# Pooling additions cut into pieces on GpSimd, and contiguous additions in place of strided sums on VectorE

## The chip, the core and the metric

One core of one Trainium2 chip runs the kernel. The metric is the device time of one execution in microseconds (us), as the median of several runs. Three runs of the kernel before gave 667.07, 664.21 and 663.7 us: median 664.21. Engines are named as in the profile: PE (TensorE matmul), PEld (its weight load), DVE (VectorE), ACT (ScalarE), POOL (GpSimd), SP (SyncE, which issues most of the DMAs).

## What is computed

An attention with pooled keys and values (8 batches, 8 heads, 576 rows, head size 64), and behind it a mixture of eight experts of which each row uses one:

```python
k_p = k.reshape(B, H, 72, 8, D).mean(axis=3)          # 576 keys -> 72 means of 8
v_p = v.reshape(B, H, 72, 8, D).mean(axis=3)
attn = softmax(q @ k_p.T / sqrt(D)); out = attn @ v_p
x = out as 4608 rows of 512
e = argmax(x @ w_gate); gate = softmax(x @ w_gate)[e]; eom = sigmoid(x @ w_output_gate)[e]
y = gate * eom * (relu(x @ w1[e]) @ w2[e])
```

The change concerns only the two `mean` lines: how the sums over eight neighbours are made.

## The kernel before

The program has two phases. In the first (`attention_and_routing`, up to about 180 us) the 4608 rows go through in 36 tiles of 128 rows, each in two half-steps `a` of four heads. All engines work as a software pipeline that is written out by hand: the main loop at L520 and below emits, for tile `i` and half `a`, the scores of tile `i` (PE, L228), the transposes of the probabilities of tile `i-2` (PE, L248), the row maxima `m` (DVE, L234), the products with the values of tile `i-3` (PE, L256), the exponentials (ACT, L239) and the normalising of tile `i-3` (DVE, L273, L279, L281). Each engine executes its own list in this order. In the second phase (`experts`, to the end) loops over the experts multiply rows by weights on PE.

A batch has 576 rows, so 4.5 tiles. For each batch `b` after the first, a table of due steps (`at(...)`, around L490) says when its side work is put into the lists: the keys are loaded (SP), pooled on POOL by `pool_k` (L170) and scaled by ACT (L179); the values are loaded into the one buffer `vt` (a part of `rows`; SP, L158), halved on POOL by `halve_v` (L185, at L188: the eight summands of 64 elements become four), then summed on DVE by `pool_v` (L190, at L191), placed by ACT (L201) and turned by PE (L206). The DVE part of the pooling goes through a queue of small steps: `pooled(b)` is a generator, and `work(n)` takes up to `n` steps from the queue's front at three places of a half-step (2, 1 and 1 steps, `WORK`). Behind it in the same queue stand the routing steps of a group of four tiles (`route`, L296 to L357): small DVE instructions on 128x32 or 128x4 elements in SBUF, among them L302, L306, L310, L314, L331 and L334, with matmuls `rk` between them. POOL's own list holds, besides the pooling, the scatters of finished rows (L390) and a few small fills.

For batch 0 nothing is halved: `first_v` has DVE sum eight summands at once, and DVE also pools its keys (`ready_k`). The list of DVE at the start is therefore keys half 0, values half 0, `m`, keys half 1, values half 1, `m`.

`vt` exists once, so SP's loads of the next values wait until DVE (or POOL) has read the old ones.

Of the kernel before, what the change touches and what calls it, by code (L numbers as in the profile page):

```python
# [15 lines left out]
ALU = mybir.AluOpType  # L16
AX = mybir.AxisListType
PSUM = bass.MemoryType.PSUM

B, H, S, D = 8, 8, 576, 64  # L20
# [49 lines left out]
def attention_and_routing(ctx, tc, sh, qT, kT, v, wg, wst, xs):  # L70
    nc = tc.nc
# [12 lines left out]
    vt = sh.rows[:, 0:6 * DM].rearrange("p (a c f) -> p a c f", a=2, c=3)  # L84
# [61 lines left out]
    k_t, vp_t, vT_t = {}, {}, {}  # L146
# [20 lines left out]
        nc.sync.dma_start(k_t[0][:, 2:4], k[:, 2:4])  # L167
        nc.sync.dma_start(q_t[0][:, :, P:S], q[:, :, P:S])

    def pool_k(b, eng, c0=0, c1=4):  # L170
        k = k_t[b][:, c0:c1]
        for w in (4, 2):
            eng.tensor_tensor(k[:, :, 0:w], k[:, :, 0:w], k[:, :, w:2 * w], op=ALU.add)
        eng.tensor_tensor(k[:, :, 0], k[:, :, 0], k[:, :, 1], op=ALU.add)

    def scale_k(b, c0=0, c1=4):
        for h in range(2):
# [3 lines left out]
    def ready_k(a):  # L181
        pool_k(0, nc.vector, 2 * a, 2 * a + 2)
        scale_k(0, 2 * a, 2 * a + 2)

    def halve_v(b):  # L185
        vp_t[b] = p2.tile([P, 3, 2, D], F32, tag="vp", name=f"vp{b}", bufs=1)
        for a in range(2):
            nc.gpsimd.tensor_tensor(vt[:, a, :, 0:256], vt[:, a, :, 0:256], vt[:, a, :, 256:512], op=ALU.add)  # L188

    def pool_v(b, a, c, n=1, w=4):  # L190
        nc.vector.tensor_reduce(vp_t[b][:, c:c + n, a], vt[:, a, c:c + n, 0:w * D].rearrange("p c (r d) -> p c d r", r=w),  # L191
                                axis=AX.X, op=ALU.add)

    def first_v(a):
        if a == 0:
            vp_t[0] = p2.tile([P, 3, 2, D], F32, tag="vp", name="vp0", bufs=1)
        pool_v(0, a, 0, 3, 8)

    def place_v(b, c):
        for h in range(2):  # L200
# [264 lines left out]
    def at(step, f, *args):  # L465
        plan.setdefault(step, []).append((f, args))

    def pooled(b):
        for a in range(2):
            for c in range(3):  # L470
                pool_v(b, a, c)
                yield 0

    tick = [0]
# [15 lines left out]
    for b in range(1, B):  # L490
        f = S * b // P + 0.5 * (b % 2)
        at(f - 8.5, load_k, b)
        at(max(f - 5, 0), load_v, b)
        at(f - 4.5, load_q, b)
        at(f - 5.5, pool_k, b, nc.gpsimd)
        at(max(f - 2.5, 1.5), scale_k, b)
        at(f - 2.5, halve_v, b)
        at(f - 2, lambda b: queue.insert(0, [pooled(b), 0, -1]), b)
        for c in range(3):
            at(f - 0.5 + 0.5 * c, place_v, b, c)  # L500
        at(f - 0.5, turn_v, b)
        at(f + 1.5, gate_v, b)
# [18 lines left out]
    prepare_counts()  # L521
    ready_k(0)
    first_v(0)
    at(-0.5, ready_k, 1)
    at(-0.5, first_v, 1)
    at(1.5, prepare_routing)
    for c in range(3):
# [603 lines left out]
def program():  # L1131
# [12 lines left out]
    with ExitStack() as st:  # L1144
# [27 lines left out]
        with tile.TileContext(nc) as tc:  # L1172
            with ExitStack() as ctx, tc.manual_schedule():
                attention_and_routing(ctx, tc, sh, qT, kT, v, wg, wst, xs)
# [24 lines left out]
```

## Time and profile before

| | us |
|---|---|
| median of 3 runs | 664.21 |
| the profiled execution, its own time | 664.95 |
| its span in the trace | 663.2 |
| PE busy in the span | 612.9 (92%) |
| DVE busy | 356.3 (54%) |
| ACT busy | 260.0 (39%) |
| POOL busy | 217.4 (33%) |
| mean granted TensorE clock | 0.98 |

The profiled execution stands 0.74 us above the median of the runs. The shares are means over the whole span; DVE and ACT work mostly in the first phase. A row of the timeline gives start, length, engine, line, operation, output and input, the count of instructions merged into it, and in brackets the idle time of the engine before it and what ended it. A row of the groups gives the count, the busy time and the mean length in ns, then the idle time. A row of the windows gives for a stretch of time each engine's busy time, then the granted TensorE clock, the DMA share and the GB/s.

### The profile page before, as it was taken

The numbers are of one execution on the slowest core, as the hardware profiler recorded it, in microseconds if no ns is written. First come the engines' busy times: TensorE is split into PE (matmuls) and PEld (weight loads), VectorE is DVE, ScalarE is ACT, GpSimd is POOL, SyncE is SP. The second block draws the span as 40 slices with busy tenths as digits, with TensorE's granted clock in tenths as the row PEclk, the third lists the DMA queues.
The fourth block names the chain that finished last, engine by engine and source line by source line (L and its number), as shares of the span: only waits on it lengthen the run. The fifth ranks groups of instructions, "written<-read, shape, count | busy, mean of one in ns | idle before, by whom it ended". The sixth has DMA issues, their size and how long they took to land.

```text
span 663.2 us, 11977 instructions
## 1 busy us (share of the span) xinstructions
PE 612.9 (92%) x3715; PEld 558.4 (84%) x3716; DVE 356.3 (54%) x877; ACT 260.0 (39%) x693; POOL 217.4 (33%) x270
## 2 busy tenths in 40 slices
PE   0898988999978999999999999999998899999996
PEld 0787877988976999899798988999897898989895
DVE  5689989899883722577546422354142722222221
ACT  2776857888541511347244301333040420211110
POOL 3547628663432321231404112131222213030213
PEclk9998988999998899999989999999999899999999
DMA  8899757883435921467746422074113102020203
GB/s 268 275 290 285 225 181 263 251 231 121 129 144 177 315 80 49 122 215 248 272 139 209 149 70 61 19 231 134 55 22 134 32 20 80 16 63 32 64 32 77
DMA packets 28746, 95.82 MB, mean 144 GB/s; under 512 B 4735, under 2 KB 5759, under 8 KB 26882
## 3 DMA queue, kind: packets, MB, share of 16 engines
q1 hardware_dynamic: 18194, 61.92, 29.5%
q0 software_dynamic: 10480, 33.13, 15.1%
q8 instruction: 21, 0.34, 0.2%
q14 instruction: 51, 0.42, 0.2%
HBM read 76.13 MB, written 20.22 MB: 145 GB/s over the span
## 4 chain that ended last, share of the span: by engine, by line
PE 66%; issue 2%; DVE 1%; DVEq 0%; POOL 0%; ACT 0%; POOLq 0%
PE p_y L849 32%; PE p_h L868 31%; PE p_x L830 2%; DVE w1a L993 1%; PE p_y L830 0%; POOL out L1110 0%; DVE rows L999 0%; DVE xt L986 0%; ACT xt L933 0%; PE p_y L910 0%; DVE sums L1019 0%; DVEq L681 0%; DVEq L1018 0%; DVEq L1030 0%; DVEq L798 0%
## 5 line engine op out<-in xcount | busy, mean ns | idle before, releaser
L948 ACT ACTIVATE ht<-p_h 128x384 fp32r<-128x384 f32 (+1 forms) x104 | 46.8, 450 | 267.0 <-PE p_h L868 266.7
L868 PE MATMUL p_h<-xt,w1b 128*128 128x384 f32 (+1 forms) x736 | 117.8, 321 | 4.1 <-issue 3.0
L868 PEld LDWEIGHTS p_h<-xt,w1b 128*128 128x128 f32 x736 | 116.6, 191 | 5.4 <-issue 3.5
L849 PE MATMUL p_y<-w2a,ht 128*128 128x512 f32 x456 | 109.1, 399 | 6.2 <-issue 4.2
L1006 DVE SCALAR_TENSOR_TENSOR ht<-p_h,ht 128x384 fp32r<-128x384 f32 (+1 forms) x104 | 52.5, 505 | 114.9 <-ACT ht L948 114.8
L849 PE MATMUL p_y<-w2b,ht 128*128 128x512 f32 x480 | 113.6, 396 | 0.0
L849 PEld LDWEIGHTS p_y<-w2a,ht 128*128 128x128 f32 x456 | 87.1, 193 | 25.0 <-issue 6.7
L849 PEld LDWEIGHTS p_y<-w2b,ht 128*128 128x128 f32 x480 | 89.8, 188 | 20.5
L868 PE MATMUL p_h<-xt,w1a 128*128 128x256 f32 (+1 forms) x640 | 95.1, 309 | 4.2 <-DVE sums L1019 4.2
L868 PEld LDWEIGHTS p_h<-xt,w1a 128*128 128x128 f32 x640 | 94.4, 193 | 5.0 <-DVE sums L1019 4.4
L999 DVE TENSOR_SCALAR rows<-p_y,sc 128x512 f32<-128x512 f32 x41 | 30.5, 749 | 122.7 <-PE p_y L849 122.7
L1110 POOL DMA_INDIRECT out<-rows,dst x41 | 41.6, 1015 | 129.7 <-DVE rows L999 124.9
L256 PE MATMUL av<-vbd,pT 128*128 128x162 f32 (+1 forms) x480 | 75.6, 313 | 8.5 <-DVE vbd L216 2.9
L239 ACT ACTIVATE p<-p_h,m 128x72 f32<-128x72 f32 x288 | 70.9, 361 | 25.4 <-DVE m L234 25.2
L256 PEld LDWEIGHTS av<-vbd,pT 128*128 128x128 f32 (+1 forms) x480 | 62.8, 185 | 11.9 <-issue 6.4
L1085 POOL DMA_INDIRECT rows<-xs,src x51 | 58.6, 1149 | 24.2 <-POOL src L1081 13.9
L1080 POOL COPY nx<-rows 128x6 f32<-128x6 f32 x17 | 3.2, 190 | 149.1 <-PE p_y L830 71.2
L390 POOL DMA_INDIRECT xs<-xg,where x36 | 36.0, 1000 | 47.2 <-DVE where L345 22.9
L228 PE MATMUL p_h<-kbd,q_even 128*128 128x144 f32 (+1 forms) x160 | 30.6, 321 | 15.7 <-DMA q_even<-qT 12.2
L249 ACT ACTIVATE pT<-ptr 128x384 f32<-128x384 f32 x72 | 37.8, 526 | 5.7 <-PE ptr L248 5.6
L228 PEld LDWEIGHTS p_h<-kbd,q_even 128*128 128x128 f32 (+1 forms) x160 | 24.5, 203 | 17.1 <-issue 12.2
L248 PE MATMUL ptr<-ident,p 128*128 128x128 f32 x216 | 37.2, 283 | 1.8 <-DVE running L333 1.7
(172 smaller groups left out, 712.2 us busy)
## 6 DMA issues: line engine op xcount, KB each, us to landing
stage<-wst SPq DMA_DIRECT2D x64, 512.0 KB, 5.3
kq<-kT SPq DMA_DIRECT2D x7, 1152.0 KB
rows<-v SPq DMA_DIRECT2D x16, 288.0 KB
kq<-qT SPq DMA_DIRECT2D x4, 1152.0 KB
q_even<-qT SPq DMA_DIRECT2D x3, 1152.0 KB
rows<-v SPq DMA_DIRECT2D x8, 256.0 KB
rows<-v SPq DMA_DIRECT2D x8, 160.0 KB
kq<-kT SPq DMA_DIRECT2D x2, 576.0 KB
```

The costliest lines, as they stand in the source:

```text
L228: nc.tensor.matmul(s[r0:r0 + n, 144 * c:144 * c + 144], q_t[b][:, 2 * a + c, s0:s0 + n], kbd[b % 2][:, 2 * a + c, :], start=True, stop=True)
L239: nc.scalar.activation(pt[i % 3][:, 4 * a + h, 0:KEYS], sv[:, h], AF.Exp, bias=m[:, h:h + 1])
L248: nc.tensor.transpose(tr[:, P * c:P * c + P], src[:, o:o + P], ident)
L249: nc.scalar.activation(pT_t[i][:, 3 * a:3 * a + 3, :], tr[:, 0:384].rearrange("p (c n) -> p c n", c=3), AF.Copy)
L256: nc.tensor.matmul(av[r0:r0 + n, COLS * c:COLS * c + 2 * COLS], pT[:, 3 * a + c, r0:r0 + n], vbd[b % 2][:, a, c].rearrange("p h f -> p (h ...
L390: ins = nc.gpsimd.indirect_dma_start(out=xs, out_offset=bass.IndirectOffsetOnAxis(ap=where, axis=0), in_=x.bitcast(I32), in_offset=None)
L849: i = mm(p_y[k], ht[:, h, f, P * k:P * k + P], w[:, part, o:o + DM], start=(f == 0 and part == 0 and h == 0), stop=(f == 7 and h == 1))
L868: i = mm(to, w[:, part, o:o + P], x, start=(d == 0 and k == 0), stop=(d == 3 and k == len(terms) - 1))
L948: act(ht[:, 0, f, 0:size * P], p_h[f % 3][:, 0:size * P], AF.Relu).then_inc(q["hh"], 1)
L1006: nc.vector.scalar_tensor_tensor(ht[:, 1, f, 0:n], src, 0.0, ht[:, 0, f, 0:n].bitcast(F32), op0=ALU.max, op1=ALU.subtract).then_inc(q["hl" ...
L1085: nc.gpsimd.indirect_dma_start(out=xb[:, k].bitcast(I32), out_offset=None, in_=xs, in_offset=bass.IndirectOffsetOnAxis(ap=src[:, k:k + 1], ...
L1110: nc.gpsimd.indirect_dma_start(out=out, out_offset=bass.IndirectOffsetOnAxis(ap=dst[:, k:k + 1], axis=0), in_=yb[k], in_offset=None, bound ...
```

## The change

`pool_k` gets an argument `apart`; with 1 (batches 1 to 7, on POOL) the first two of its three levels are issued for one of the four column groups at a time, 288 and 144 elements in place of 1152 and 576. `halve_v` is issued for each third of the values, 256 elements in place of 768. `pool_v` no longer sums four summands by a strided `tensor_reduce`, three instructions for a half of the heads; it adds contiguous halves of the buffer by two `tensor_tensor` instructions (384 and 192 elements), the first of them in place. `first_v` uses three of these (768, 384, 192 elements). The queue item `pooled(b)` has four steps in place of six.

```diff
-    def pool_k(b, eng, c0=0, c1=4):
-        k = k_t[b][:, c0:c1]
-        for w in (4, 2):
-            eng.tensor_tensor(k[:, :, 0:w], k[:, :, 0:w], k[:, :, w:2 * w], op=ALU.add)
-        eng.tensor_tensor(k[:, :, 0], k[:, :, 0], k[:, :, 1], op=ALU.add)
+    def pool_k(b, eng, c0=0, c1=4, apart=0):
+        for w in (4, 2, 1):
+            n = apart if apart and w > 1 else c1 - c0
+            for c in range(c0, c1, n):
+                k = k_t[b][:, c:c + n]
+                eng.tensor_tensor(k[:, :, 0:w], k[:, :, 0:w], k[:, :, w:2 * w], op=ALU.add)
...
         for a in range(2):
-            nc.gpsimd.tensor_tensor(vt[:, a, :, 0:256], vt[:, a, :, 0:256], vt[:, a, :, 256:512], op=ALU.add)
-
-    def pool_v(b, a, c, n=1, w=4):
-        nc.vector.tensor_reduce(vp_t[b][:, c:c + n, a], vt[:, a, c:c + n, 0:w * D].rearrange("p c (r d) -> p c d r", r=w),
-                                axis=AX.X, op=ALU.add)
+            for c in range(3):
+                nc.gpsimd.tensor_tensor(vt[:, a, c, 0:256], vt[:, a, c, 0:256], vt[:, a, c, 256:512], op=ALU.add)
+
+    def pool_v(b, a, n):
+        to = vt[:, a, :, 0:n] if n > D else vp_t[b][:, :, a]
+        nc.vector.tensor_tensor(to, vt[:, a, :, 0:n], vt[:, a, :, n:2 * n], op=ALU.add)
...
-        pool_v(0, a, 0, 3, 8)
+        for n in (4 * D, 2 * D, D):
+            pool_v(0, a, n)
...
-            for c in range(3):
-                pool_v(b, a, c)
+            for n in (2 * D, D):
+                pool_v(b, a, n)
                 yield 0
...
-        at(f - 5.5, pool_k, b, nc.gpsimd)
+        at(f - 5.5, pool_k, b, nc.gpsimd, 0, 4, 1)
```

In the new file L191 becomes L194, L188 becomes L190, L173 and L174 become L175, and the lines below stand three further down (L331 becomes L334).

First place, POOL's list in the attention phase, from the keys of batch 2 to the values of batch 2 (`kq` are the keys, `rows` the values, `xg` a group's rows). Before:

```order
L173 TENSOR_TENSOR kq<-kq 128x4x288
L173 TENSOR_TENSOR kq<-kq 128x4x144
L174 TENSOR_TENSOR kq<-kq 128x4x72
L268 IOTA xg_499 128x4
L188 TENSOR_TENSOR rows<-rows 128x3x256 x2
```

and now:

```order
L175 TENSOR_TENSOR kq<-kq 128x288 x4
L175 TENSOR_TENSOR kq<-kq 128x144 x4
L175 TENSOR_TENSOR kq<-kq 128x4x72
L271 IOTA xg_517 128x4
L190 TENSOR_TENSOR rows<-rows 128x256 x6
```

Nothing has changed places; five instructions have become fifteen. The 144-element pieces each wait for their own 288-element piece, the last level for all of them; the six pieces of the values wait for nothing that POOL does.

Second place, DVE's list where the values of batch 2 are pooled, in the middle of the routing of the first group (`vp` are the pooled values, `gden` and `pos` belong to the routing, `m`, `grec`, `xg`, `graw` to the tiles). Before:

```order
L234 TENSOR_REDUCE m_0_560<-p_h 128x4
L191 TENSOR_REDUCE vp_517<-rows 128x64 x2
L273 RECIPROCAL grec_501<-av_0_564 128x4
L191 TENSOR_REDUCE vp_517<-rows 128x64
L279 TENSOR_TENSOR xg_499<-av_0_564,grec_501 128x256
L281 TENSOR_TENSOR graw_498<-av_0_564,grec_501 128x64
L191 TENSOR_REDUCE vp_517<-rows 128x64
L234 TENSOR_REDUCE m_1_584<-p_h 128x4
L191 TENSOR_REDUCE vp_517<-rows 128x64 x2
L273 RECIPROCAL grec_501<-av_1_588 128x4
L326 TENSOR_REDUCE gden_599<-ex_489 128x4
```

and now:

```order
L237 TENSOR_REDUCE m_0_582<-p_h 128x4
L194 TENSOR_TENSOR rows<-rows 128x3x128
L194 TENSOR_TENSOR vp_535<-rows 128x3x64
L276 RECIPROCAL grec_519<-av_0_586 128x4
L194 TENSOR_TENSOR rows<-rows 128x3x128
L282 TENSOR_TENSOR xg_517<-av_0_586,grec_519 128x256
L284 TENSOR_TENSOR graw_516<-av_0_586,grec_519 128x64
L194 TENSOR_TENSOR vp_535<-rows 128x3x64
L237 TENSOR_REDUCE m_1_606<-p_h 128x4
L329 TENSOR_REDUCE gden_614<-ex_507 128x4
L333 TENSOR_TENSOR pos_617<-rk_608,running 128x32
```

The pooling of a batch now ends in the half-step in which it begins, and the routing steps behind it stand two steps of the queue earlier. The step that first reads the second half of the heads (the second `rows<-rows`) stands in front of that half-step's `xg`; before, the fourth reduce did, behind `xg`.

## The prediction

> **What bounds the kernel now.** First the windows, to see where the change can matter. It touches the attention phase alone, so I compare that phase with the long one behind it:
>
> ```profile
> 20.00:165.00 145.00, 131.62 (x1028) 120.78 (x1029) 129.55 (x454) 112.35 (x424) 84.91 (x69) 0.96 0.75 238
> 200.00:663.00 463.00, 447.33 (x2474) 405.21 (x2473) 184.76 (x281) 125.89 (x216) 112.36 (x156) 0.98 0.35 112
> ```
>
> From 200 us on PE is busy for 447 of 463 us; nothing there changes, so time saved earlier shifts this part as a whole. From 20 to 165 us PE (first busy figure) and DVE (third) are both nearly full, 131.6 and 129.6 of 145 us. Two full engines do not each cost their whole time: DVE costs only where PE runs dry. The waits of PE in these 145 us show how much that is:
>
> ```profile
> PE av L256 <- DVE vbd L216: 2.9, 1, 2.9
> PE av L256 <- DVE grec__3_1365 L339: 1.9, 1, 1.9
> PE ptr L248 <- DVE running L333: 1.7, 1, 1.7
> PE av L256 <- DVE graw L281: 1.6, 2, 1.1
> PE av L256 <- DVE zr L316: 1.5, 2, 1.1
> ```
>
> These are 9.6 us, all for DVE. They are few and long, so the next question is what DVE did just before. The longest, in the timeline, with the clock granted after it and after two others (the figure before the last two):
>
> ```profile
> 81.11 3.57 POOL L188 TENSOR_TENSOR rows<-rows 128x768 f32<-128x768 f32 x2
> 81.42 3.31 DVE L310 TENSOR_TENSOR oh<-cand,best 128x32 bf16<-128x32 f32 x1
> 85.74 1.04 PE L256 MATMUL av<-vbd,pT 128*64 128x162 f32 x10 [2.91 <-DVE vbd L216]
> 57.00:60.00 3.00, 3.00 (x16) 2.99 (x15) 2.56 (x11) 2.48 (x10) 2.37 (x3) 0.58 1.10 214
> 87.00:90.00 3.00, 3.00 (x22) 2.79 (x23) 1.37 (x6) 2.28 (x8) 0.00 (x0) 0.50 0.27 100
> 111.00:114.00 3.00, 3.00 (x17) 2.27 (x16) 2.97 (x12) 2.15 (x9) 2.04 (x3) 0.50 0.23 88
> ```
>
> L310 handles 32 elements and lasts 3.31 us: it ends with POOL's pair of additions (81.11 + 3.57 = 84.68). PE then starves for 2.91 us, and behind the gap TensorE runs at half clock. The three windows lose 3 x (0.42 + 0.50 + 0.50) = 4.3 us of PE time. So these long DVE instructions cost twice. How much of DVE's time is such waiting, the groups of the phase show; the last row is the same shape with one operand in PSUM, which never stretches:
>
> ```profile
> L331 DVE TENSOR_SCALAR gden<-gden 128x4 f32<-128x4 f32 x7 | 6.2, 879 | 0.0
> L310 DVE TENSOR_TENSOR oh<-cand,best 128x32 bf16<-128x32 f32 x7 | 6.1, 874 | 0.2
> L302 DVE TENSOR_TENSOR d<-lg,mx 128x32 f32<-128x32 f32 x7 | 3.7, 527 | 0.0
> L306 DVE SCALAR_TENSOR_TENSOR cand<-d,rev 128x32 f32<-128x32 f32 x7 | 3.7, 525 | 0.0
> L314 DVE TENSOR_TENSOR zs<-lg,oh 128x32 f32<-128x32 f32 x7 | 2.9, 410 | 0.0
> L330 DVE TENSOR_TENSOR pos<-rk,running 128x32 f32<-128x32 f32 x7 | 1.3, 181 | 0.1
> ```
>
> At 181 ns each the 35 instructions of the first five rows would take 6.3 us; they take 22.6. So 16.3 us of DVE time is waiting for POOL.
>
> **Pieces on POOL.** A waiting DVE instruction can get in where POOL goes from one instruction to the next. Whether it does, three cases show, and a fourth what a short wait costs:
>
> ```profile
> 44.71 1.82 POOL L188 TENSOR_TENSOR rows<-rows 128x768 f32<-128x768 f32 x1 [6.91 <-DMA rows<-v]
> 44.90 1.68 DVE L310 TENSOR_TENSOR oh<-cand,best 128x32 bf16<-128x32 f32 x1
> 52.65 2.62 POOL L173 TENSOR_TENSOR kq<-kq 128x1152 f32<-128x1152 f32 x1 [4.35 <-DMA kq<-kT]
> 53.95 1.34 DVE L331 TENSOR_SCALAR gden<-gden 128x4 f32<-128x4 f32 x1
> 106.09 3.58 POOL L188 TENSOR_TENSOR rows<-rows 128x768 f32<-128x768 f32 x2
> 105.72 3.99 DVE L331 TENSOR_SCALAR gden<-gden 128x4 f32<-128x4 f32 x1
> 65.32 1.38 DVE L306 SCALAR_TENSOR_TENSOR cand<-d,rev 128x32 f32<-128x32 f32 x1
> ```
>
> At 44.90 L310 came through after the first of two additions (44.71 + 1.82 = 46.53, L310 ends 46.58). At 53.95 L331 came through behind the first level of the keys, where POOL's next instruction waits for that one. At 81.42 and 105.72 DVE had to wait for both. So between POOL instructions that do not depend on each other, two cases stand against one; I take a chance of one half at each such border. At 65.32 a wait of 1.2 us opened no gap on PE: a delay of about 1 us is covered by the half-step that PE has in hand.
>
> The price of the pieces, from POOL's rows:
>
> ```profile
> L173 POOL TENSOR_TENSOR kq<-kq 128x1152 f32<-128x1152 f32 x7 | 18.5, 2637 | 20.2 <-DMA kq<-kT 20.1
> L173 POOL TENSOR_TENSOR kq<-kq 128x576 f32<-128x576 f32 x7 | 9.9, 1408 | 0.6
> L174 POOL TENSOR_TENSOR kq<-kq 128x288 f32<-128x288 f32 x7 | 5.6, 796 | 0.5
> ```
>
> 1152 against 576 elements gives 2.13 ns an element and 0.18 us an instruction. A piece of 256 then takes 0.73, of 288 0.80, of 144 0.49 us. The values of a batch become 6 x 0.73 = 4.4 in place of 3.57 us, the keys 4 x 0.80 + 4 x 0.49 + 0.80 = 6.0 in place of 4.8. POOL's 85 us in 145 become about 98, no bound. A DVE instruction that arrives at random waits 0.4 us to the next border and, at a chance of one half, on average one more piece: about 1.1 us, in place of up to 3.8. That is at the edge of what is covered. [...] I take the middle: of the 9.6 us of gaps 3 stay (**-6.6**), and of the 4.3 us of half clock, which only the long gaps brought, 1 stays (**-3.3**).
>
> **Sums on VectorE.**
>
> ```profile
> L191 DVE TENSOR_REDUCE vp<-rows 128x64 f32<-128x256 f32 x42 | 23.9, 596 | 2.6 <-POOL rows L188 2.6
> L191 DVE TENSOR_REDUCE vp<-rows 128x192 f32<-128x1536 f32 x2 | 5.5, 2756 | 4.9 <-DMA rows<-v 4.9
> L173 DVE TENSOR_TENSOR kq<-kq 128x576 f32<-128x576 f32 x2 | 1.5, 747 | 0.0
> L173 DVE TENSOR_TENSOR kq<-kq 128x288 f32<-128x288 f32 x2 | 0.9, 458 | 0.1
> ```
>
> The last two rows are additions of two SBUF operands: 1.0 ns an element and 0.17 us each. So 384 elements take 0.55, 192 take 0.36, 768 take 0.94 us. A batch costs 2 x (0.55 + 0.36) = 1.8 in place of 6 x 0.596 = 3.6 us; seven batches give DVE 12.3 us back. Most of this is covered: in the half-steps with pooling PE mostly stays busy, and the gaps of the list above that pooling has a part in (L281 and L316) are counted already. I give it nothing more.
>
> At the start it is on the path. The rows, with SP's load of the next values:
>
> ```profile
> 16.98 2.29 PE L228 MATMUL p_h<-kbd,q_even 128*128 128x144 f32 x8 [3.46 <-ACT kbd L179]
> 18.95 1.15 SPq L158 DMA_DIRECT2D rows<-v  x3
> 29.89 0.31 PE L228 MATMUL p_h<-kbd,kq 128*64 128x144 f32 x1 [2.13 <-ACT p L239]
> ```
>
> PE waits at 16.98 for the second half of the keys, which DVE pools behind the first 2.76 us reduce; SP's loads at 18.95 wait for the second reduce, and the queries of batch 1 stand behind these loads in SP's queue, so PE's wait at 29.89 (the ACT instruction named had ended; the tile comes by DMA) moves with them. Each reduce becomes 0.94 + 0.55 + 0.36 = 1.85 us, 0.9 less. Of 1.8 us I take **-1.5**, since the first saving may end in a wait for the scores or the keys.
>
> What it costs. The old reduces read one tensor and were left alone by POOL; the new additions read two from SBUF, like the instructions that wait. These rows show a reduce in the midst of POOL's key additions, and batch 1, where DVE waited for POOL's values:
>
> ```profile
> 70.46 4.14 POOL L173 TENSOR_TENSOR kq<-kq 128x1152 f32<-128x1152 f32 x2 [3.81 <-DMA kq<-kT]
> 70.95 0.58 DVE L191 TENSOR_REDUCE vp<-rows 128x64 f32<-128x256 f32 x1
> 27.47 1.80 POOL L188 TENSOR_TENSOR rows<-rows 128x768 f32<-128x768 f32 x1 [3.30 <-DMA rows<-v]
> 29.31 1.12 DVE L191 TENSOR_REDUCE vp<-rows 128x64 f32<-128x256 f32 x2 [2.42 <-POOL rows L188]
> ```
>
> [...]
>
> In the batches whose pooling meets the next keys, each addition may wait a piece or two, 0.4 to 1.1 us, four times: then it costs as much as the reduce did. In batch 1 the second half of the heads now stands ahead of `xg`, and POOL delivers it 4.4 us after it starts instead of 3.6; `m` behind it is 1 to 2 us later than at present. Bounds of all this: nothing (all covered) and 3 us; I take **+1.3**.
>
> **Sum.** -6.6 - 3.3 - 1.5 + 1.3 = -10.1. The profiled execution took 664.95 us, 1.75 of it outside its span: 654.9. It lies 0.74 above the median of the runs, by which it would be 654.1. I give 654.5.
>
> **The rivals.** [...] Chance 0.09.
>
> *It cancels* (no change). DVE waits less at a time but oftener; the new additions pay at POOL's pieces what they save, and the gaps fall only to 7 of 9.6 us with the clock still dropping. -2.6 - 1 - 1.5 + 3 = -2: 662.5. For it: 35 instructions stay exposed and 28 are added. Chance 0.13.
>
> *Another supply is late next* (faster, less). The gap before the half clock of 57 us falls where the DMA engines are full (share 1.10 in that window, 0.27 and 0.23 in the other two). Without it the keys and values may come late instead, so that the gaps up to there, L333 and about half of L281 and L316, some 3 us, stay with their 1.3 of clock. Then -10.1 + 4 = -6: 658.5. Chance 0.20.
>
> **How the numbers follow.** The forecast case, 648 to 657, has 0.58. About 0.5% (3.3 us) is what a measurement of this kernel can tell from no change, so faster means under 660.9: 0.58 + 0.20 = 0.78. The cancelling case gives 0.13 for the same, the port rival 0.09 for slower. The low end takes all gaps, all clock and 1.8 at the start, at no cost: 664.2 - 9.6 - 4.3 - 1.8 = 648.5. The high end reaches to the cancelling case, 662.5, and leaves the slower rival out.
>
> **What would show it.** Right: L334 and L313 (before L331, L310) with a longest duration below 2 us; no PE gap above 1.5 us between 40 and 160 us; granted clock 1.0 from 85 to 115 us; the two first sums of values 1.9 us each, and SP's second set of value loads near 17.3 us. Wrong: DVE instructions of 4 us and more on small tiles; the new L194 rows well above 0.55 and 0.36 us; or PE gaps that now end in a DMA.

## The result, and the profile after

The changed kernel takes 662.07 us (median; 659.41 to 664.46) beside 665.57 for the kernel before on the same chip: ratio 0.9944, with an interval of 0.9924 to 0.9964. On two other chips it came out at 0.9907 (0.9879 to 0.9936) and 0.9884 (0.9839 to 0.9930). So it is faster, by 3.5 to 5.6 us; the forecast was 10. Its profiled execution took 662.01 us, with a span of 660.2.

The window from 20 to 165 us as before (after the times: PE, PEld, DVE, ACT, POOL; then granted clock, DMA share, GB/s), and the waits of PE in it:

```profile
20.00:165.00 145.00, 129.59 (x1034) 120.58 (x1033) 117.91 (x443) 112.88 (x424) 98.37 (x139) 0.95 0.75 239
```

```profile
PE av L259 <- DVE cand L309: 6.8, 3, 4.0
PE p_h L231 <- DMA kq<-qT: 3.9, 1, 3.9
...
PE ptr L251 <- DVE vbd L219: 0.7, 1, 0.7
PE av L259 <- DVE vbd L219: 0.5, 1, 0.5
```

DVE has 11.6 us less to do (117.9 against 129.6), yet PE's waits for DVE are 6.8 + 0.7 + 0.5 = 8.0 us, where 3 were forecast and 9.6 stood before, and a wait of 3.9 us for a transfer has come. The clock is 0.95 against 0.96. The gain was there for a time, and was given back. The 18th addition `xg` of DVE shows that, first of the kernel before, then of the changed one:

```profile
67.86 0.42 DVE L279 TENSOR_TENSOR xg<-av,grec 128x256 f32<-128x256 f32 x1
```

```profile
58.43 0.42 DVE L282 TENSOR_TENSOR xg<-av,grec 128x256 f32<-128x256 f32 x1
```

A lead of 9.4 us, at 58 us of the trace. Behind a wait of PE for the queries it falls to 1.9 at the 25th; by the 40th, where the kernel before has had its own long stalls, it is back at 10.4 us. At the 49th it is 4.9, at the 67th (169.45 against 170.75) 1.3. The rows of PE where it is lost, with the blocks of POOL and the row of DVE behind them:

```profile
65.69 0.47 PE L231 MATMUL p_h<-kbd,kq 128*64 128x144 f32 x1 [3.91 <-DMA kq<-qT]
```

```profile
107.62 5.70 POOL L175 TENSOR_TENSOR kq<-kq 128x288 f32<-128x288 f32 x9
109.04 3.01 DVE L305 TENSOR_TENSOR d<-lg,mx 128x32 f32<-128x32 f32 x1
112.66 1.07 PE L259 MATMUL av<-vbd,pT 128*128 128x162 f32 x6 [1.81 <-DVE cand L309]
127.05 0.97 POOL L393 DMA_INDIRECT xs<-xg,where  x1 [0.30 <-issue]
128.04 5.67 POOL L175 TENSOR_TENSOR kq<-kq 128x288 f32<-128x288 f32 x9
127.97 4.49 DVE L305 TENSOR_TENSOR d<-lg,mx 128x32 f32<-128x32 f32 x1
133.06 1.96 PE L259 MATMUL av<-vbd,pT 128*128 128x162 f32 x6 [3.99 <-DVE cand L309]
```

L305 is one of the small routing instructions (32 elements), and it is stretched as L310 and L331 were before, but now by the nine pieces of the keys. At 127.97 it asks just before a scatter ends, and does not come through until 132.46. The pieces follow each other by 0.75 and 0.45 us (the tests below have them apart), so the eighth of the nine begins at 128.04 + 4 x 0.75 + 3 x 0.45 = 132.39: DVE was let in there, and at no border before, three ahead of 288-element pieces and three ahead of 144-element ones. The `xg` behind it on DVE waits, to 111.97 and 132.38 us, so PE's product `av`, for which the program has two buffers, starts only behind gaps of 1.81 and 3.99 us. In the windows behind the gaps of 3.91 and 3.99 us the clock is 0.50; from 85 to 115 us, where the gap of 1.81 lies, it is 1.00:

```profile
66.00:69.00 3.00, 3.00 (x19) 2.54 (x16) 1.96 (x8) 1.19 (x5) 0.27 (x1) 0.50 0.47 152
85.00:115.00 30.00, 28.19 (x234) 27.22 (x233) 28.00 (x104) 23.14 (x91) 23.91 (x34) 1.00 0.76 238
135.00:138.00 3.00, 3.00 (x18) 2.93 (x17) 1.89 (x9) 3.00 (x14) 0.00 (x0) 0.50 0.38 150
```

The groups of DVE in 20 to 165 us (count, then busy time, mean ns, idle time before):

```profile
L194 DVE TENSOR_TENSOR rows<-rows 128x384 f32<-128x384 f32 x14 | 9.4, 670 | 5.9 <-POOL rows L190 5.9
L305 DVE TENSOR_TENSOR d<-lg,mx 128x32 f32<-128x32 f32 x7 | 8.5, 1217 | 0.0
L194 DVE TENSOR_TENSOR vp<-rows 128x192 f32<-128x192 f32 x14 | 7.0, 499 | 0.2
L317 DVE TENSOR_TENSOR zs<-lg,oh 128x32 f32<-128x32 f32 x7 | 2.2, 308 | 0.0
L313 DVE TENSOR_TENSOR oh<-cand,best 128x32 bf16<-128x32 f32 x7 | 1.9, 267 | 0.2
L309 DVE SCALAR_TENSOR_TENSOR cand<-d,rev 128x32 f32<-128x32 f32 x7 | 1.4, 196 | 0.0
L334 DVE TENSOR_SCALAR gden<-gden 128x4 f32<-128x4 f32 x7 | 1.2, 169 | 0.0
```

The other four of the five shapes that lost 16.3 us before are nearly free (6.7 us for 28 instructions; they took 18.9). L305 has taken over: 8.5 us, of which the two rows above are 7.5.

The executions of one kernel differ more than the ratio of two kernels (659.4 to 664.5 here), so a trace shows a mechanism, and the times of many runs show what it is worth. From the 67th `xg` to the end of the span, where both kernels run the same instructions, the kernel before takes 492.5 us and the changed one 490.8, but the traces of this case range from 489.3 to 497.8: a lead at the 67th is not yet a gain at the end.

### The profile page after: what moved, and what is told of

It reads as the page before. It is cut to its first block, busy times and chain, and to the rows that moved or that the text cites. A ratio compares the mean times of both kernels' runs of the same rounds, so it can differ in the third digit from the quotient of the medians.

```text
span 660.2 us, 12038 instructions
## 1 busy us (share of the span) xinstructions
PE 608.9 (92%) x3715; PEld 556.5 (84%) x3716; DVE 342.6 (52%) x867; ACT 260.2 (39%) x693; POOL 231.3 (35%) x340
## 4 chain that ended last, share of the span: by engine, by line
PE 66%; issue 2%; DVE 1%; DVEq 0%; POOL 0%; ACT 0%; POOLq 0%
PE p_y L852 32%; PE p_h L871 31%; PE p_x L833 2%; DVE w1a L996 1%; PE p_y L833 0%; POOL out L1113 0%; DVE rows L1002 0%; DVE xt L989 0%; ACT xt L936 0%; PE p_y L913 0%; DVE sums L1022 0%; DVEq L684 0%; DVEq L1021 0%; DVEq L1033 0%; DVEq L801 0%
## 5 line engine op out<-in xcount | busy, mean ns | idle before, releaser
L871 PE MATMUL p_h<-xt,w1b 128*128 128x384 f32 (+1 forms) x736 | 116.4, 318 | 4.5 <-issue 3.6
L871 PEld LDWEIGHTS p_h<-xt,w1b 128*128 128x128 f32 x736 | 115.2, 188 | 5.8 <-issue 4.0
L175 POOL TENSOR_TENSOR kq<-kq 128x288 f32<-128x288 f32 (+1 forms) x63 | 39.5, 659 | 21.9 <-DMA kq<-kT 18.4
```

The costliest lines, as they stand in the source:

```text
L871: i = mm(to, w[:, part, o:o + P], x, start=(d == 0 and k == 0), stop=(d == 3 and k == len(terms) - 1))
```

## The experiments

### Each half alone

The sums alone are the old file with the new `pool_v` (two or three contiguous additions) and GpSimd's additions whole; the pieces alone are the new file with the old sums:

```diff
+    def pool_v(b, a, n):
+        to = vt[:, a, :, 0:n] if n > D else vp_t[b][:, :, a]
+        nc.vector.tensor_tensor(to, vt[:, a, :, 0:n], vt[:, a, :, n:2 * n], op=ALU.add)
```

> The kernel before with the contiguous sums on VectorE alone (and at the start), GpSimd's additions undivided. Theory that the pieces did the work and late supply and the keys' pieces ate it: this half gives the 1.5 us of the start and little else, 662 to 665 beside a kernel before at 665.6, since the four additions of a batch now wait for whole GpSimd blocks of 1.8 and 2.6 us. Rival, that the whole gain of the changed kernel is the start and the shorter sums: as fast as the changed kernel, 661 to 662.5.

> The changed kernel's pieces on GpSimd, with the strided sums of before on VectorE. If the pieces did the work and the gain was lost again: it has a lead over the kernel before of 5 us and more by 60 us of the trace, loses it at the queries of batch 3 and at the keys' pieces behind a scatter, and ends 1 to 3 us ahead (662.5 to 664.5). If the gain is the sums and the start alone: within 1 us of the kernel before, no lead at 60 us beyond 1 us.

Measured on one chip: the sums alone 665.77 us, ratio 1.0014 (0.9988 to 1.0041); the pieces alone 659.64, ratio 0.9932 (0.9908 to 0.9956). The gain is that of the pieces. The sums are worth nothing by themselves, less than I had left them, and the rival that put the gain in them falls. The pieces alone did better than expected (662.5 to 664.5). Both traces are those of the fastest of twelve executions (658.70 and 657.00 us), and both have a lead of 7.4 us at the 67th `xg`, the sums alone too, whose median gains nothing. So a lead in one trace may be that execution's.

### The keys' pieces in chained order

The same nine instructions for the keys, but each 144-element piece directly behind its own 288-element piece, whose end it must then really wait for:

```diff
     def pool_k(b, eng, c0=0, c1=4, apart=0):
-        for w in (4, 2, 1):
-            n = apart if apart and w > 1 else c1 - c0
-            for c in range(c0, c1, n):
-                k = k_t[b][:, c:c + n]
-                eng.tensor_tensor(k[:, :, 0:w], k[:, :, 0:w], k[:, :, w:2 * w], op=ALU.add)
+        n = apart or c1 - c0
+        order = [(w, c, n) for c in range(c0, c1, n) for w in (4, 2)] + [(1, c0, c1 - c0)]
+        for w, c, m in order:
+            k = k_t[b][:, c:c + m]
+            eng.tensor_tensor(k[:, :, 0:w], k[:, :, 0:w], k[:, :, w:2 * w], op=ALU.add)
```

> The changed kernel with the same fifteen GpSimd instructions, but a column group's 144-element addition directly behind its own 288-element one, for which it has to wait. Theory that VectorE is not let in between additions behind a scatter that do not wait for each other: no L305 above 1.5 us at 109 and 128 us, the gaps of TensorE at 112.66 (1.81) and 133.06 (3.99) and their half clock gone; 5 to 7 us less than the changed kernel, 655 to 657. Theory that the lead is lost to the late queries and to what is late next: the long L305 may go, but the time stays within 1.5 us of the changed kernel (660.5 to 662.5).

657.06 us beside 665.08: ratio 0.9880 (0.9848 to 0.9913). The same place in its trace, with the row of the groups and the waits of PE in 20 to 165 us:

```profile
123.43 0.97 POOL L393 DMA_INDIRECT xs<-xg,where  x1 [0.30 <-issue]
124.34 0.94 DVE L305 TENSOR_TENSOR d<-lg,mx 128x32 f32<-128x32 f32 x1
124.43 6.65 POOL L175 TENSOR_TENSOR kq<-kq 128x288 f32<-128x288 f32 x9
125.90 1.06 PE L259 MATMUL av<-vbd,pT 128*128 128x162 f32 x6 [0.44 <-DVE cand L309]
```

```profile
L305 DVE TENSOR_TENSOR d<-lg,mx 128x32 f32<-128x32 f32 x8 | 3.2, 396 | 0.0
```

```profile
PE p_h L231 <- DMA kq<-qT: 3.8, 2, 2.9
PE av L259 <- DVE graw L284: 1.5, 3, 0.6
PE av L259 <- DVE cand L309: 1.4, 2, 1.0
```

L305 again asks just before the scatter ends. Now it comes through at the first border, 0.94 us later (4.49 before), and PE waits 0.44 us. PE's waits for DVE are 2.9 us in all, the 3 of the forecast. The lead at the 67th `xg` is 10.1 us, where the changed kernel had 1.3.

Since the ratio came out differently on three chips (0.9944, 0.9907 and 0.9884 above), the changed kernel and the chained order were also run side by side:

> The changed kernel itself once more, as the measure for the two below on the same chip: 0.5 to 0.9% below the kernel before.

> The chained order of the keys' pieces again, beside the changed kernel on the same chip. Theory that blocks which stay shut cost the gain: 0.4 to 0.7% (3 to 5 us) below the changed kernel of this call. Rival, that the first result was the chip's: within 0.2% of it.

664.31 us (0.9884, 0.9839 to 0.9930) and 658.45 us (0.9826, 0.9782 to 0.9870): the medians of this chip stand 5.9 us apart, 0.6% by the ratios. The two intervals overlap, but five of the six chained runs are faster than all six of the changed kernel. So the chained order is worth about as much as the change itself gained there (5.6 us). That it does so by opening the shut blocks is read from the traces: in the four traces with the chained order, no small instruction of the routing lasts longer than 0.95 us. The long row is no accident of one execution either. Two further traces of the changed kernel have it at the same place:

```profile
130.27 4.03 DVE L305 TENSOR_TENSOR d<-lg,mx 128x32 f32<-128x32 f32 x1
```

```profile
128.24 4.48 DVE L305 TENSOR_TENSOR d<-lg,mx 128x32 f32<-128x32 f32 x1
```

The row of 3.01 us at 109.04 is shorter there, 1.04 and 1.34 us. The three traced executions of the changed kernel stand at the median of their runs (662.01 us) or are the longest of six (664.88 and 669.17), so whether its faster executions have the long row is not shown. The first of the two rows is from this run, which served as the measure on its chip (661.01 us, 0.9907):

> The changed kernel itself, beside the next two and the kernel before on the same chip, as the measure for them: 0.56% below the kernel before, as already measured.

### The expert weights later

The six early loads of expert weights, 3 MB, go out between 22 and 39 us, while the DMA engines are full (a share of 0.99 in these 17 us of the changed kernel's trace, 0.98 in the kernel before). Here they go out later:

```diff
     for c in range(STAGES):
-        at(3 + 0.5 * c, stage_in, c)
+        at(20 + 2 * c, stage_in, c)
```

> The changed kernel with the six early loads of expert weights (512 KB each) put off from 22 to 39 us to about 85 to 125 us, where the DMA engines are less full. Theory of late supply: the queries of batch 3 land before TensorE wants them, the wait of 3.91 us at 65.69 and the half clock to 72 us go (3.4 us more), the lead of 8 to 9 us over the kernel before lives past 72 us; some of it is still lost at the long L305 of 109 and 128 us. 655 to 658. Theory that only the keys' pieces behind a scatter cost the gain: the wait goes but the time stays within 1.5 us of the changed kernel (660.5 to 663).

> The changed kernel with the later weights again, beside the changed kernel on the same chip. If the late queries cost it 5 us: 0.6 to 0.8% below. With the kernel before, the two runs gave 0.36 and 0.81%; if that is what the weights cost any version, the changed kernel gains 0.4 to 0.8% too, and late supply is no loss that the change brought.

> The kernel before with the six early loads of expert weights put off, as in the run with the changed kernel. Theory of late supply behind the changed kernel's lead: the kernel before has no lead that could run into the queries, so it gains little, 663.5 to 666 beside 665. Rival, that the early weights cost any version some 5 us: 659 to 661.

> The kernel before with the weights later, once more, since its first run (ratio 0.992) came out otherwise than the theory of late supply said and its trace did not show where. Theory that the early weights cost both kernels the same: again 0.7 to 0.9% below the kernel before, faster than the changed kernel of the same call. Theory that only a kernel with a lead gains: within 0.3% of the kernel before.

The changed kernel: 656.96 us, ratio 0.9870 (0.9847 to 0.9893), and on the chip where the changed kernel itself stood at 0.9884, 663.20 us, 0.9864 (0.9811 to 0.9916). The kernel before: 667.05 beside 670.62, 0.9919 (0.9883 to 0.9954), and 663.59 beside 666.10, 0.9964 (0.9937 to 0.9991). In the traces the wait for the queries shrinks from 3.9 to 1.1 and 0.9 us. But what the later loads are worth, 0.2% with the change on the same chip (0.7% if ratios of two chips are compared) and 0.4 to 0.8% without it, does not tell the two kernels apart. My expectation that the kernel before would gain nothing was wrong, and so was the 0.6 to 0.8% that I expected of the second run. That the crowded transfers ate this change's gain is not shown. Nor does the time of a run follow from the long rows alone: the first trace with the change and the later loads still has L305 at 4.47 and 3.47 us (656.96 us in the median), the second has none above 1.8 us (663.20, on another chip). Where the kernel before gains its part, its two traces do not show: their 67th `xg` stands 0.4 and 1.2 us later than in the kernel before.

### What shuts a block

Two edits leave the keys' order as changed and put something between: a small iota between the scatter and the pieces, or a no-operation between the pieces:

```diff
+        if apart:
+            nc.gpsimd.iota(apart_t, pattern=[[1, 4]], base=0, channel_multiplier=0, allow_small_or_imprecise_dtypes=True)
...
+                if apart and c:
+                    nc.gpsimd.nop()
```

> The changed kernel with one small GpSimd instruction (an iota of 128x4) ahead of the keys' pieces, so that none of these blocks stands directly behind a scatter. Theory that the scatter right ahead is what keeps VectorE out of the pieces that follow: the long L305 of 3.0 and 4.5 us go and the time falls as with the chained order, 656 to 658.5. Theory that it is the missing wait between the pieces, whatever stands ahead: long L305 or their like stay, 660.5 to 663.

> The changed kernel with a no-operation of GpSimd between the keys' pieces of a level (the order unchanged). If any instruction that makes GpSimd's queue stop opens the border: no L305 above 1.5 us, 0.5% below the changed kernel, as with the chained order. If only a wait for an unfinished instruction opens it: long L305 stay, within 0.2% of the changed kernel.

The iota: 665.14 us beside 670.62, ratio 0.9886 (0.9845 to 0.9927), as the changed kernel, and the long row is still there, right through the iota and the pieces:

```profile
131.49 4.58 DVE L308 TENSOR_TENSOR d<-lg,mx 128x32 f32<-128x32 f32 x1
131.56 0.15 POOL L173 IOTA apart_t<- 128x4 f32 x1
```

So the scatter need not stand directly ahead. (The changed kernel did not run on this chip; 0.9886 compares with its 0.9884 to 0.9944 on three others.) The no-operations: 659.60 us, 0.9917 (0.9884 to 0.9950), beside 0.9907 for the changed kernel on that chip. Its trace has no long `d`, but the instruction `oh` at 110.08 was held 1.54 us, over three of the 144-element pieces. The lead is 7.8 us at the 67th `xg`; the traced execution (657.58 us) keeps it, the median of the runs does not. This one is inconclusive.

Then the hand-over by itself, in a test that stands ahead of the whole changed kernel:

```diff
+        for kind in "ABCDEFFEDCBA":
+            nc.gpsimd.tensor_copy(t, at_[7][:, 0, 0:32])
...
+            for m, w in todo_:
+                k = at_[m]
+                if kind == "F":
+                    nc.gpsimd.nop()
+                nc.gpsimd.tensor_tensor(k[:, 0:w], k[:, 0:w], k[:, w:2 * w], op=ALU.add)
+            for n in range(16):
+                nc.vector.tensor_tensor(u[:, 32 * n:32 * n + 32], t, t, op=ALU.add)
```

> The changed kernel with a test ahead of it: twelve blocks of eight GpSimd additions of 288 elements (or four of 288 and four of 144), each beside a stream of 16 VectorE additions of 128x32 elements, two tensor_reduce between any two of them. Kinds in the order A B C D E F F E D C B A: A independent additions; B the same directly behind a scatter; C behind a scatter and a small iota; D behind a scatter, each 144-element addition directly behind its 288-element one (a true wait); E behind a scatter, four of 288 and then four of 144 as in the changed kernel; F behind a scatter, independent, with a no-operation ahead of each. Theory of the missing wait: in A, B, C and E one VectorE addition lasts nearly as long as the block (4 to 6 us), in D one is let in every 1.25 us (288 + 144), F open. Theory of the scatter: A and C let one in at each border (0.75 us), B and E none.

Blocks of kind D and E first, then the two passes of kind B, then C in its second pass:

```profile
37.28 5.30 POOL L130 TENSOR_TENSOR kq<-kq 128x288 f32<-128x288 f32 x8
38.25 0.45 DVE L132 TENSOR_TENSOR stage<-stage 128x32 f32<-128x32 f32 x1
38.81 0.64 DVE L132 TENSOR_TENSOR stage<-stage 128x32 f32<-128x32 f32 x1
45.80 4.82 POOL L130 TENSOR_TENSOR kq<-kq 128x288 f32<-128x288 f32 x8
48.30 1.93 DVE L132 TENSOR_TENSOR stage<-stage 128x32 f32<-128x32 f32 x1
```

```profile
17.21 6.01 POOL L130 TENSOR_TENSOR kq<-kq 128x288 f32<-128x288 f32 x8
17.32 5.20 DVE L132 TENSOR_TENSOR stage<-stage 128x32 f32<-128x32 f32 x1
102.08 6.04 POOL L130 TENSOR_TENSOR kq<-kq 128x288 f32<-128x288 f32 x8
102.35 0.63 DVE L132 TENSOR_TENSOR stage<-stage 128x32 f32<-128x32 f32 x1
90.45 6.45 DVE L132 TENSOR_TENSOR stage<-stage 128x32 f32<-128x32 f32 x1
```

In D, where each small piece really waits, DVE came in at every border, more often than expected (0.64 and 0.45 us in turn). In E it came in between the 288-element pieces, but at 48.30 it was kept out by the 144-element ones, whose wait had long been met: 1.93 us, three borders. The second pass of E has the same 1.93. B and C were shut in one pass (5.20 and 6.45 us) and open in the other; A and F were open in both. Both theories fall in part: independent pieces can be open without any wait, and a scatter ahead does not by itself shut them. Kind E always stood behind a scatter, so this test does not tell what its 144-element pieces do without one.

What differs between the two passes of B is when DVE asks: 0.11 us behind the block's start, or 0.27. So the last test varies that alone: three additions of DVE in a block, the first held back by a count of short instructions.

```diff
+        for late in (10, 14, 16, 17, 18, 19, 20, 21, 22, 24, 28, 32):
+            for kind in "ABFE":
...
+                for h in range(late - 8 * (kind == "A")):
+                    nc.vector.tensor_reduce(r[:, h:h + 1], t, axis=AX.X, op=ALU.add)
+                for n in range(3):
+                    nc.vector.tensor_tensor(u[:, 32 * n:32 * n + 32], t, t, op=ALU.add)
```

> The changed kernel with another test ahead of it: 48 blocks of eight GpSimd additions, each beside only three VectorE additions of 128x32 elements (two tensor_reduce between any two), the first of which is held back by 10 to 32 short tensor_reduce, so that it arrives from within the scatter up to 1.5 us into the block. Kinds in turn: A independent additions, no scatter; B directly behind a scatter; F behind a scatter with no-operations between; E behind a scatter, four of 288 and four of 144. Theory that a whole block is open or shut, and that the moment of VectorE's arrival decides: some B rows of 4 to 5 us and others of at most 0.75 us, by arrival; A and F open at all arrivals. Theory that each border opens by chance: rows of 1 to 3 us mixed among all kinds.

```profile
14.21 6.02 POOL L126 TENSOR_TENSOR kq<-kq 128x288 f32<-128x288 f32 x8
14.32 5.21 DVE L130 TENSOR_TENSOR stage<-stage 128x32 f32<-128x32 f32 x1
42.53 0.73 DVE L130 TENSOR_TENSOR stage<-stage 128x32 f32<-128x32 f32 x1
```

Of the 108 additions of DVE in kinds A, B and F, 107 lasted at most 0.76 us, one border. The one exception, 5.21 us, came again 0.11 us behind the start of a block behind a scatter; at 0.16 us (42.53, in the block that starts at 42.37) the block was open. In kind E, all four additions that asked within the last 288-element piece were held 1.92 or 1.93 us, over three borders. So nothing here looks like a chance per border. Behind a scatter, waits met in advance shut the small pieces every time, independent 288-element pieces are open nearly always, and an arrival 0.11 us behind the start of such a block met six shut borders at once, twice. In the real kernel L305 arrived 0.07 us ahead of the block at 127.97 and at 128.24; but it was kept out at 130.27 too, 0.39 us behind the block's start (129.88), and at 109.04, 1.42 us behind. What shut the 288-element borders there stays open.

What the tests leave out, the kernels' own traces show. Where POOL had been idle before a block, the same pieces in the same order let DVE in. In the trace of the pieces alone, one block of each sort (L341 and L312 are small instructions of the routing):

```profile
69.76 5.72 POOL L175 TENSOR_TENSOR kq<-kq 128x288 f32<-128x288 f32 x9 [2.34 <-DMA kq<-kT]
72.03 0.80 DVE L341 SCALAR_TENSOR_TENSOR grec__1_910<-ez,gden 128x4 f32<-128x4 f32 x1
126.61 0.97 POOL L392 DMA_INDIRECT xs<-xg,where  x1 [0.31 <-issue]
127.61 5.75 POOL L175 TENSOR_TENSOR kq<-kq 128x288 f32<-128x288 f32 x9
130.55 1.54 DVE L312 TENSOR_TENSOR oh<-cand,best 128x32 bf16<-128x32 f32 x1
```

L341 asked in the last 288-element piece and came in ahead of the first 144-element piece (69.76 + 4 x 0.75 = 72.76), although that piece's wait had long been met. Behind the scatter, L312 asked at nearly the same place of the block and was held over three 144-element pieces. Eight traces have the keys' pieces level by level (three of the changed kernel, the pieces alone, two with later weights, the iota, the no-operations). In their blocks that begin behind an idle wait, all 32 rows that DVE had to hold came in at the next border, seven of them ahead of one of the first three 144-element pieces. In their blocks behind a scatter (with the iota between or not), none came in there: 19 rows were held over one or more of these pieces, and each came in ahead of the fourth, the eighth instruction of the block. So neither a wait met in advance nor a scatter shuts the small pieces by itself; the shut ones had both. No run takes the scatter away from the same block, and why it matters stays open.

### Both remedies

The chained order and the later weights together, once with the new sums and once with the old:

> The changed kernel with both: the keys' pieces in chained order and the weights later. If the queries and the keys' pieces each cost their part of the lead, the two gains (5 us each against the changed kernel) add up but for what is late next: 650 to 654. If there is a third limit right behind either (the same 657 in both runs by chance of the same next wait): 655.5 to 657.5.

> As the run with chained keys and later weights, but with VectorE's strided sums of before. Theory that the contiguous sums save VectorE time that is off the path, and pay at GpSimd's pieces what they save: within 1.5 us of that run. Theory that they help once the other stalls are gone: 2 to 4 us above it. The start alone would make it 1.0 to 1.5 us slower.

658.22 us beside 670.62, ratio 0.9823 (0.9792 to 0.9853), and 658.55, 0.9841 (0.9803 to 0.9878). Together they gain 1.6 to 1.8%, but not clearly more than the chained order alone on the chip where it did best (0.9826). The new sums make no difference that these runs can tell.

## Why the prediction was wrong

**What bounds the kernel** was read rightly: the waits of PE behind DVE's waits for POOL. Where POOL's pieces let DVE in, the gaps went, and the lead of 9.4 us at 58 us is what the forecast expected of the whole phase.

**The step that failed is the chance of one half at each border**, with its "on average one more piece: about 1.1 us". It took the borders of all independent pieces as equal and each as a draw of its own, on two cases against one. In the rows themselves the two shut cases stand directly behind a scatter (as here, ahead of the pair at 81.11), and the open one, 44.90, behind an idle wait of 6.91 us:

```profile
80.08 0.99 POOL L390 DMA_INDIRECT xs<-xg,where  x1 [0.16 <-issue]
```

Over the four traces with undivided values (the kernel before, the sums alone, two with later weights), seven rows of DVE that met such a pair directly behind a scatter waited for both additions, and four that met one behind an idle wait or an iota came in between. In the changed kernel the borders of the values were open (L313, L317 and L334 fell to 267, 308 and 169 ns; no row was held over one in its three traces). Those of the keys were not. Behind four 288-element pieces, the waits of the 144-element pieces have long been met (1.35 to 2.25 us earlier, at 0.75 and 0.45 us a piece), and where such a block followed a scatter, DVE was kept out of the first three every time. Before, POOL's second instruction for the keys had to wait for its first, and L331 came in at that border (53.95); cutting both levels, level by level, replaced one true wait by four that are met in advance. I had noted that each 144-element piece waits for its own 288-element piece, and had not asked whether it would still be waiting. The chained order has the same pieces and true waits: the forecast came out there (ratio 0.9880 and 0.9826, 8 and 11 us; 2.9 us of gaps, where I had put 3), with some luck, since its trace also has 3.8 us of waits for the queries that the sum leaves out. How much of the missing 5 to 6 us the shut borders cost is not measured apart from that order.

**Term by term.** *Gaps of PE*, -6.6: only 9.6 - 8.0 = 1.6 us of waits for DVE went, and 3.9 for the queries came. *Half clock*, -3.3: nothing; the clock that I expected at 1.0 from 85 to 115 us was there, but two new dips follow the gaps of 3.91 and 3.99 us. *Start*, -1.5: the first sums and the loads behind them came as worked out:

```profile
15.16 1.54 DVE L194 TENSOR_TENSOR rows<-rows 128x768 f32<-128x768 f32 x2
16.74 0.36 DVE L194 TENSOR_TENSOR vp<-rows 128x192 f32<-128x192 f32 x1
17.13 1.15 SPq L158 DMA_DIRECT2D rows<-v  x3
```

1.54 + 0.36 = 1.90 us (1.85 forecast), loads at 17.13 (17.3 forecast), and the first `xg` 1.1 us ahead (0.6 and 0.8 in the two further traces). With the sums alone no such gain reaches the end. *Cost of the new additions*, +1.3: 670 and 499 ns in place of 0.55 and 0.36 us, 14 x (0.12 + 0.14) = 3.6 us of DVE's time, and 5.9 us of waits for POOL's rows; what reaches the path is not separable from the start's gain, and together they are nothing (1.0014).

**The rivals.** *The slower rival* (0.09): that DVE is kept out at the borders of a block is what happens in the keys' blocks behind a scatter, for 4.49 us in the row at 127.97, but not everywhere, and the kernel did not become slower (0.9944). That a port is behind it, no run shows; the rows show only how long DVE was held, and at which borders. That only a true wait opens a border fits the chained order, which waits and was open (0.95 us at most), and the waits met in advance behind a scatter (19 rows held); it does not fit the independent 288-element pieces, open in 107 of 108 rows, nor the small pieces behind an idle wait (7 rows). *Another supply is late next* named the right transfer (the queries, 3.9 us), but the later weights are worth as much to the kernel before, so that it is not shown to be where the gain went. Its reading of the DMA share was taken behind the gaps: the gap that ends at 85.74 lies itself in a window (84 to 87 us) with a share of 1.00, as full as the one ahead of 57 us (0.97). *It cancels* gave 662.5, near the result, but by luck, from costs that did not arise: the small instructions did not wait oftener, one of them waited long.

**What was named as a sign** came out accordingly: L334 and L313 short, clock and loads right; DVE rows of 4 us on a small tile, L194 rows above 0.55 and 0.36 us and a gap that ends in a DMA, all named as signs of a wrong forecast, are there, and so are gaps of PE above 1.5 us between 40 and 160 us (3.91, 1.81 and 3.99), of which a right one was to have none.

## What to carry to other kernels

When a GpSimd block is cut so that VectorE can get in, look at each border and ask what GpSimd waits for there at that moment, and what stands ahead of the block. Here a wait for the instruction just ahead opened the border every time, behind a scatter too (no row above 0.95 us in the chained order, 0.45 and 0.64 in kind D); behind a scatter, a wait that had long been met left it shut (19 rows, and 1.92 us in kind E). Put dependent pieces directly one behind the other, not level by level. And look for the next small instruction that meets the block, since a stall can move from one routing step to another (L310 and L331 to L305), with 8.0 of 9.6 us of gaps left.

## What the runs showed of the hardware that was not expected

- A VectorE instruction of 32 elements was kept out for 4.49 us over six borders between GpSimd instructions, and came in ahead of the eighth; in the tests alike (5.20 and 5.21 us, before the eighth of eight pieces).
- The same small pieces, with their waits met in advance, let VectorE in at the next border behind an idle wait (7 rows) and not at one of the first three behind a scatter (19 rows).
- Of the requests that met a block behind a scatter just after its start, the two at 0.11 us were held 5.20 and 5.21 us, the three at 0.16 us no longer than 0.74.
- Six loads of 512 KB that the changed kernel first uses at 126.57 us go out from 22 us on. Putting them off gained 0.4 and 0.8% for the kernel before, and 0.2% for the changed kernel on the same chip, less than its interval can tell.
